# A packed attention layout without copies, moved slots, late coefficients and earlier branch hints in a fused attention and two-layer kernel

## The chip, the core and the metric

The kernel runs on one core of one Trainium2 chip. The metric is device time in microseconds (us) of one execution; lower is better. The kernel before takes 646.76 us, the median of three runs (646.42 to 647.4).

## What is computed

```python
# q, k, v: 2 x 8 heads x 768 x 64; window 128, 4 sinks
keep = (pos < n_sink) | ((rel >= 0) & (rel < window))       # rel = query - key
a = softmax(where(keep, q @ k.T / 8, -1e9)); x = a @ v       # -> 1536 x 512
g = relu(x @ w_in) ** 2;  y = g @ w_out                      # first layer, d_ff 2048
h = y @ w2_in                                                # second layer
P = a0 + a1*h + a2*h**2 + a3*h**3
Q = 1 + |b0|*|h| + |b1|*h**2
out = (P / (Q + 1e-6)) @ w2_out
```

## The kernel before

**Units and groups.** Attention is cut into 24 units: two heads (one per half of the partitions) by two query blocks of 128. `GROUPS` makes four groups of tokens, of 512, 256, 256 and 512 columns, with 8, 4, 4 and 8 units. A query block is worked on in two halves of 64 queries (j = 0, 1), and each half sees a row of 224 columns: 192 keys and 32 sink keys. `pack_attention` writes, on the host, one block of inputs for each unit, in which the keys of each half stand in the order in which the half uses them (so many keys stand twice), and V stands as pieces of 128 rows: `va` for the first 128 columns of each half and `vb` for the rest. The first unit of a sequence (`blk0 == 0`) has one plain block of 128 and one such block.

**A unit's work** (`att_unit`). Scores S are eight small matmuls (L301); VectorE adds the mask and finds the extreme of each row (L310); ScalarE exponentiates (L312); VectorE and GpSimd normalize (L320); TensorE transposes T (L333); ScalarE and VectorE copy the transposes out (L335); then O, the product with V (L348): for each job of 64 queries one matmul per head, 16 in a unit with `blk0 > 0`, 10 in the others. The trace has two records for each of these fp32 matmuls. Between these steps the generator yields.

**Order.** A planner with a timeline model orders each engine's instructions; an instruction may be drawn ahead of the program's order when it is ready and its engine has room. TensorE's order is written by hand in the start and in groups 0 to 2 (`manual_schedule`, `PINNED`); the first group's eight units run ahead of everything else, with parts of the first two gemm1 steps between them. Then `group(g)` runs 16 steps f of the first layer for one group: gemm1 (L414 to 416), `act1` (L423 to 426), and with a lag of two steps gemm2 (L437, L438, L443). The units of the next group are woven in through `slot(k)`, called three times a step: `slot` calls `tick()`, and a tick advances every open unit by one yield and on each third tick opens a new one. In group 0 the ticks begin after slot 6 (`first = 6`). In these steps the score banks are PSUM banks 6 and 7, and the third gemm1 step (f = 2) of group 0 uses bank 6 too. gemm1 otherwise alternates between banks 4 and 5, so that step f needs the `act1` of step f - 2 done.

**Weights** come as 64-bit floats into three `st` buffers (L130) and are converted on ScalarE and VectorE (L139, L140, L398, L399). All loads of weights, keys and V are issued by SyncE (SP) in its queue's order; the load of V waits in that queue for the unit before to finish with its buffer (one buffer each for `va` and `vb`).

**Setup and end.** `setup` builds three masks from `n_sink` and `window`, which a small load brings (`nsw`, L195); the coefficients a and b come by two more small loads on ScalarE's queue (L196, L197), and three VectorE instructions (L595 to L597) work them up. They are used from the second layer on (`rational`, L144). The second layer runs 3 times 16 steps with a lag of three; its `act2` is a chain over ScalarE, VectorE and GpSimd (L149 to L159, L464, L465). After the last output each engine reads a flag and branches past a slow general version (L983, L984). `hints()` (L792) marks, for each engine, a hint that this branch is likely taken, behind the last instruction of that engine in the second layer; SyncE's comes behind the stores of the second of the three token blocks.

Of the kernel before, what the change touches and what calls it, by code (L numbers as in the profile page):

```python
# [10 lines left out]
F32 = mybir.dt.float32  # L11
# [8 lines left out]
P = 128  # L20
# [6 lines left out]
KP = 2 * WK + NSK  # L27
# [61 lines left out]
def pack_attention(q, k, v):  # L89
# [3 lines left out]
    for g, c, seg, _ in units():  # L93
        b, blk0, nb = seg
        first = 0 if blk0 > 0 else 2
        kq, va, vb = [], [], []
        for half in range(2):
            h = 2 * c + half
            cols = []
            for n in range(first, 2 * nb, 2):  # L100
                s = blk0 * P - P + n * D
                cols += [kT[b, h][:, s : s + WK], kT[b, h][:, :NSK], kT[b, h][:, s + D : s + D + WK]]
            cols.append(qT[b, h][:, blk0 * P : (blk0 + nb) * P])
            kq.append(np.concatenate(cols, axis=1))
        heads = [v[b, 2 * c + half] for half in range(2)]
        pad = np.zeros((NSK, D), v.dtype)
        if blk0 == 0:
            va += [x[:P] for x in heads]
        for n in range(first, 2 * nb):
            s = blk0 * P - P + n * D  # L110
            for x in heads:
                w = x[s : s + WK]
                rows = np.concatenate([w, x[:NSK]] if n % 2 == 0 else [x[:NSK], w], axis=0)
                va.append(rows[:P])
                vb.append(np.concatenate([pad, rows[P:]], axis=0))
        parts += [np.concatenate(kq, axis=0).reshape(-1), np.concatenate(va, axis=1).reshape(-1),
                  np.concatenate(vb, axis=1).reshape(-1)]
# [44 lines left out]
class Fast:  # L162
# [17 lines left out]
    def setup(self):  # L180
# [11 lines left out]
        ab = c.tile([P, 6], F32, name="ab")  # L192
        self.ab = ab
# [31 lines left out]
        v.tensor_scalar_add(rel[hi_], rel[hi_], float(NSK - D))  # L225
# [8 lines left out]
        v.tensor_copy(m2[hi_, :NSK], out[hi_, :NSK])  # L234
        v.tensor_copy(m1, m2)
        v.tensor_copy(m2[lo_, WK:], out[lo_, :NSK])
        v.tensor_tensor(m1[lo_, :NSK], m1[lo_, :NSK], out[lo_, :NSK], op=ALU.max)
        v.memset(m1[lo_, WK:], -BIG)
# [11 lines left out]
    def att_load(self, u, early, alt):  # L250
# [7 lines left out]
        self.nc.sync.dma_start(raw, self.io["att"][off : off + P * w].rearrange("(p w) -> p w", w=w))  # L258
        return raw

    def att_load_v(self, u, alt):
# [3 lines left out]
        out = []  # L265
        for n, name, tag in ((wa, "va", tags[3]), (wb, "vb", tags[4])):
            t = self.att_tile(name, n, alt=tag)
            self.nc.sync.dma_start(t, self.io["att"][off : off + P * n].rearrange("(p w) -> p w", w=n))
            off += P * n
            out.append(t)  # L270
        return out
# [6 lines left out]
    def att_unit(self, u, raws, alt):  # L278
# [49 lines left out]
        pieces = [os[i] for i in range(nb)] + [os[i] + P - NSK for i in heads]  # L328
# [11 lines left out]
        jobs = [(va, 0, 0, 0, P)] if ws[0] == P else []  # L340
        for x, i in enumerate(heads):
            for j in range(2):
                y, q0 = 2 * x + j, i * P + j * D
                jobs.append((va, y + nb - len(heads), q0, q0, D))
                jobs.append((vb, y, (nb + x) * P + j * D, q0, D))
# [133 lines left out]
    def run(self, ctx):  # L479
# [16 lines left out]
        self.lastO = {}  # L496
# [145 lines left out]
        def second(which, g, f, between=None):  # L642
# [23 lines left out]
            else:  # L666
                self.gemm2b(f, gg, acc)
                if f == NF - 1:
                    for t in range(TG2 // P):
# [13 lines left out]
                        else:  # L683
                            (A.copy if t % 2 == 0 else V.tensor_copy)(o, acc[t])
                            self.lastO[g == NT2 - 1] = nc.sync.dma_start(dst, o)
# [4 lines left out]
        def group(g):  # L690
# [3 lines left out]
            if last:  # L694
# [5 lines left out]
                self.flag()  # L700
                wload(1, 3)
# [6 lines left out]
            def slot(k):  # L708
                nonlocal pos
                first = 6 if g == 0 else -2  # L710
# [4 lines left out]
            for f in range(NF):  # L715
                if g == 0 and f < HEAD:
# [44 lines left out]
        nsec = 0  # L761
        for i in range(len(steps) + 1):
# [29 lines left out]
    def hints(self):  # L792
        E = mybir.EngineType
        for engine, op in ((E.Activation, self.lastG), (E.Pool, self.lastL), (E.DVE, self.lastR),
                           (E.PE, self.lastM), (E.SP, self.lastO[False])):
# [3 lines left out]
    def split_y(self, t, c, ys, ysp):  # L799
# [5 lines left out]
        for g, n in enumerate(GN):  # L805
# [7 lines left out]
            self.nc.gpsimd.tensor_tensor(ylo[:, c, dst], ys[g][:, c, src], yhi[:, c, dst].bitcast(F32), op=ALU.subtract)  # L813

# [20 lines left out]
class General:  # L835
# [4 lines left out]
    def segments(self):  # L840
        off, out = 0, {}
        for g, c, seg, _ in units():
            wk, wq, wa, wb = seg_dims(seg)
            views = []
            for w in (wk + wq, wa, wb):
                views.append(self.io["att"][off : off + P * w].rearrange("(p w) -> p w", w=w))
                off += P * w
            kq, va, vb = views
            b, blk0, nb = seg
            for i in range(nb):  # L850
                whole = blk0 == 0 and i == 0
                k0 = 0 if whole else (i if blk0 > 0 else 0) * KP + WK + NSK + D
# [167 lines left out]
```

## Time and profile before

| | us |
| --- | --- |
| median of three runs | 646.76 |
| the profiled execution | 643.87 |
| its span, first to last instruction | 642.1 |

| engine | busy us | share of the span |
| --- | --- | --- |
| TensorE matmul (PE) | 609.9 | 95% |
| VectorE (DVE) | 417.8 | 65% |
| ScalarE (ACT) | 417.6 | 65% |
| GpSimd (POOL) | 109.9 | 17% |

The profile's page gives shares over the whole span; the stages differ, so the readings below are taken by stretches of time. The mean granted TensorE clock is 0.997 of full speed. Loads move 60.14 MB in all. In the rows, "[x <-y]" is idle time of the engine just before an instruction and what ended it.

### The profile page before, as it was taken

How to read it: one execution, taken by the hardware profiler on the slowest of the kernel's cores; microseconds unless marked ns; L12 is line 12 of the kernel's file. 1: busy time of each engine (PE TensorE's matmuls, PEld its weight loads, DVE VectorE, ACT ScalarE, POOL GpSimd, SP SyncE). 2: the span in 40 equal slices, each digit the busy share in tenths (PEclk: the TensorE clock that was granted, in tenths of full speed). 3: DMA queues.
4: the chain of work that ended last, by engine and by line, in shares of the span. 5: the costliest groups of instructions: out<-in, count | busy, mean ns of one | idle time of the engine just before them, and what ended most of it. 6: DMA issues, size and time to landing. Idle time of an engine off the chain costs nothing.

```text
span 642.1 us, 10520 instructions
## 1 busy us (share of the span) xinstructions
PE 609.9 (95%) x3937; PEld 510.3 (79%) x3937; DVE 417.8 (65%) x852; ACT 417.6 (65%) x896; POOL 109.9 (17%) x123
## 2 busy tenths in 40 slices
PE   3677999999999999999999999999999999999995
PEld 2555777787999899998888888888888888888884
DVE  5876788623243354346666569998788787877772
ACT  3668888735454555456777768787676666766662
POOL 1220000000000011021000003443233332222221
PEclk9999999999999999999999999999999999999998
DMA  8945677621232243104565500000010000100002
GB/s 277 353 142 169 235 252 267 207 88 43 78 91 69 97 141 94 42 1 129 185 190 190 191 0 2 1 0 1 0 67 1 1 0 1 66 0 2 1 1 70
DMA packets 21947, 60.14 MB, mean 94 GB/s; under 512 B 2816, under 2 KB 5120, under 8 KB 21888
## 3 DMA queue, kind: packets, MB, share of 16 engines
q1 hardware_dynamic: 21312, 59.25, 27.4%
q8 instruction: 33, 0.54, 0.4%
q10 hardware_dynamic: 576, 0.14, 0.1%
q14 instruction: 26, 0.21, 0.1%
HBM read 56.24 MB, written 3.15 MB: 92 GB/s over the span
## 4 chain that ended last, share of the span: by engine, by line
PE 83%; ACT 8%; DVE 6%; issue 2%; DMA 1%; POOL 0%; POOLq 0%; DVEq 0%
PE b L414 13%; PE b L415 12%; PE b L416 12%; PE b L476 7%; PE b L475 7%; PE b L474 7%; PE b L437 6%; PE b L443 6%; PE b L438 6%; PE b L348 3%; ACT p L312 3%; PE b L301 2%; PE b L333 2%; ACT top L139 2%; DVE wt L140 1%
## 5 line engine op out<-in xcount | busy, mean ns | idle before, releaser
L414 PE MATMUL b<-xhi,whi 128*128 128x512 f32 (+1 forms) x320 | 112.8, 354 | 0.5 <-ACT xhi L353 0.5
L415 PE MATMUL b<-xlo,whi 128*128 128x512 f32 (+1 forms) x320 | 111.0, 347 | 0.0
L416 PE MATMUL b<-xhi,wlo 128*128 128x512 f32 (+1 forms) x320 | 111.0, 347 | 0.0
L426 DVE TENSOR_TENSOR glo<-b,ghi 128x512 fp32r<-128x512 f32 (+1 forms) x64 | 35.5, 555 | 80.5 <-ACT b L425 75.2
L437 PE MATMUL b<-ghi,whi 128*128 128x512 f32 (+1 forms) x256 | 83.6, 343 | 0.7 <-ACT ghi L424 0.7
L438 PE MATMUL b<-ghi,wlo 128*128 128x512 f32 (+1 forms) x256 | 81.9, 336 | 0.0
L465 POOL TENSOR_TENSOR glo<-t,ghi 128x512 fp32r<-128x512 f32 x34 | 45.0, 1324 | 212.9 <-ACT ghi L464 186.5
L475 PE MATMUL b<-wlo,ghi 128*128 128x512 f32 x192 | 74.7, 389 | 0.0
L474 PE MATMUL b<-whi,ghi 128*128 128x512 f32 x192 | 74.4, 389 | 0.0
L476 PE MATMUL b<-whi,glo 128*128 128x512 f32 x192 | 71.9, 389 | 0.0
L414 PEld LDWEIGHTS b<-xhi,whi 128*128 128x128 f32 x320 | 60.4, 189 | 10.1 <-issue 1.8
L312 ACT ACTIVATE p<-p,mn 128x224 f32<-128x224 f32 (+1 forms) x96 | 44.0, 459 | 34.6 <-DVE mn L310 34.6
L416 PEld LDWEIGHTS b<-xhi,wlo 128*128 128x128 f32 x320 | 60.5, 189 | 7.5
L415 PEld LDWEIGHTS b<-xlo,whi 128*128 128x128 f32 x320 | 60.5, 189 | 7.3
L320 POOL TENSOR_SCALAR p<-p,sums 128x224 f32<-128x224 f32 (+1 forms) x48 | 25.5, 542 | 234.5 <-DVE sums L316 148.6
L399 DVE TENSOR_TENSOR wlo<-wt,whi 128x512 fp32r<-128x512 f32 x64 | 44.8, 700 | 27.1 <-ACT whi L398 26.7
L398 ACT CAST whi<-wt 128x512 fp32r<-128x512 f32 x64 | 39.5, 617 | 32.8 <-PE b L415 21.1
L423 ACT ACTIVATE b<-b 128x512 f32<-128x512 f32 (+1 forms) x64 | 31.1, 488 | 45.2 <-PE b L416 45.2
L443 PE MATMUL b<-glo,whi 128*128 128x512 f32 (+1 forms) x256 | 56.2, 342 | 0.0
L437 PEld LDWEIGHTS b<-ghi,whi 128*128 128x128 f32 x256 | 48.4, 189 | 8.1 <-issue 1.7
L438 PEld LDWEIGHTS b<-ghi,wlo 128*128 128x128 f32 x256 | 48.5, 190 | 4.9
L139 ACT CAST top<-st 128x512 f16<-128x512 bf16 x64 | 49.7, 777 | 1.8 <-DVE wt L140 1.8
(126 smaller groups left out, 1264.0 us busy)
## 6 DMA issues: line engine op xcount, KB each, us to landing
st<-w SPq DMA_DIRECT2D x64, 512.0 KB, 3.6
raw<-att SPq DMA_DIRECT2D x12, 544.0 KB, 3.6
va<-att SPq DMA_DIRECT2D x16, 256.0 KB, 3.0
vb<-att SPq DMA_DIRECT2D x16, 256.0 KB, 3.9
raw_e<-att SPq DMA_DIRECT2D x4, 544.0 KB, 6.7
out<-o SPq DMA_DIRECT2D x8, 256.0 KB, 2.0
raw<-att SPq DMA_DIRECT2D x6, 336.0 KB, 3.7
va<-att SPq DMA_DIRECT2D x8, 192.0 KB, 3.8
```

What stands on the lines that cost most here:

```text
L139: nc.scalar.copy(top.bitcast(F16).rearrange("p (n w) -> p n w", w=2)[:, :, 1], head)
L312: self.lastA = A.activation(p, p, AF.Exp, scale=-1.0, bias=mn, accum_out=sums[:, k * nb + i : k * nb + i + 1])
L414: nc.tensor.matmul(h[:, :n], whi[:, cs], xhi[:, c, :n], start=(c == 0), stop=False)
L415: nc.tensor.matmul(h[:, :n], whi[:, cs], xlo[:, c, :n], start=False, stop=False)
L416: nc.tensor.matmul(h[:, :n], wlo[:, cs], xhi[:, c, :n], start=False, stop=(c == NC - 1))
L437: nc.tensor.matmul(acc[m], whi[:, ms], ghi, start=(f == 0 and not pk), stop=pk, **kw)
L438: nc.tensor.matmul(acc[m], wlo[:, ms], ghi, start=False, stop=pk, **kw)
L443: nc.tensor.matmul(acc[m], whi[:, ms], glo, start=False, stop=pk or f == NF - 1, **kw)
L465: self.lastL = nc.gpsimd.tensor_tensor(glo, t3, ghi.bitcast(F32), op=ALU.subtract)
L474: nc.tensor.matmul(acc[t], ghi[:, ts_], whi, start=(f == 0), stop=False)
L475: nc.tensor.matmul(acc[t], ghi[:, ts_], wlo, start=False, stop=False)
L476: self.lastM = nc.tensor.matmul(acc[t], glo[:, ts_], whi, start=False, stop=(f == NF - 1))
```

## The change

- **Keys** are stored once for a unit, with the 32 sinks between neighbouring blocks, so that a half's 224 columns are a window into the row: at `i * KB + j * D`, with KB = 160. A unit's key and query load shrinks from 544 to 352 KB (from 336 to 272 KB where `blk0 == 0`). The masks follow: three small additions to `rel` in place of one, and the sink columns move.
- **V** is stored as whole blocks (`va`) and mixed pieces (`vb`): 448 KB in place of 512 KB (256 in place of 320). A unit with `blk0 > 0` has 14 matmuls at L348 in place of 16, since one job of 128 queries takes the place of two of 64; the others 8 in place of 10. In groups 1 to 3 V comes as one load, into one of two buffers.
- **Slots**: `first` goes from 6 to 9 in group 0. The ticks then fall on slots 12, 14, 17, 19, 22, ... in place of 9, 12, 14, 17, 20, ...; the last one stays on slot 46.
- **a and b** are loaded by `coefficients()`, called at the beginning of group 3, on SyncE's queue; the three VectorE instructions move there too.
- **Hints**: SyncE's comes in step 12 of group 0, behind the key load that was traced last; ScalarE's and VectorE's in step 20 of the second layer's 48; GpSimd's and TensorE's stay at the last step.
- `General` reads the new layout; it does not run with these inputs.

```diff
-KP = 2 * WK + NSK
+KB = P + NSK
@@ seg_dims
-    return (2 * KP, nb * P, 4 * P, 4 * P) if blk0 > 0 else (KP, nb * P, 3 * P, 2 * P)
+    return (2 * KB + P, nb * P, 3 * P, 4 * P) if blk0 > 0 else (KB + P, nb * P, 2 * P, 2 * P)
@@ key_cols
-    return (i if blk0 > 0 else 0) * KP + j * WK, WQ
+    return (i if blk0 > 0 else 0) * KB + j * D, WQ
@@ setup
-        nc.scalar.dma_start(ab[:, 0:4], io["a"].partition_broadcast(P))
-        nc.scalar.dma_start(ab[:, 4:6], io["bb"].partition_broadcast(P))
...
-        v.tensor_scalar_add(rel[hi_], rel[hi_], float(NSK - D))
+        for rows, cs, x in ((lo_, slice(KB, WQ), NSK), (hi_, slice(0, D), -D), (hi_, slice(D + NSK, WQ), NSK - D)):
+            v.tensor_scalar_add(rel[rows, cs], rel[rows, cs], float(x))
@@ att_load_v
+        if alt:
+            out = [self.att_tile("va", wa, alt=tags[3]), self.att_tile("vb", wb, alt=tags[4])]
...
+        t = self.att_tile("vv", wa + wb, bufs=2)
+        self.nc.sync.dma_start(t, src)
+        return [t[:, :wa], t[:, wa:]]
@@ att_unit
-        pieces = [os[i] for i in range(nb)] + [os[i] + P - NSK for i in heads]
+        pieces = [os[i] + x for i in range(nb) for x in ((0, P - NSK) if i in heads else (0,))]
...
+        if blk0 > 0:
+            jobs = [(va, 0, 0, 0, D), (vb, 0, P, 0, D), (vb, 1, D, D, D), (va, 1, P + D, D, P)]
+        else:
+            jobs = [(va, 0, 0, 0, P + D)]
+        y, pp = 2 * len(heads) - 2, (len(pieces) - 2) * P
+        jobs += [(vb, y, pp + P, P, D), (vb, y + 1, pp + D, P + D, D), (va, len(heads), pp + P + D, P + D, D)]
@@ run
-        V.tensor_scalar(self.nabs, self.ab[:, 4:6], -1.0, None, op0=ALU.mult)
-        V.tensor_tensor(self.nabs, self.nabs, self.ab[:, 4:6], op=ALU.max)
-        V.tensor_scalar(self.ab[:, 0:4], self.ab[:, 0:4], -1.0, None, op0=ALU.mult)
...
                 self.flag()
+                self.coefficients()
                 wload(1, 3)
...
-                first = 6 if g == 0 else -2
+                first = 9 if g == 0 else -2
...
+                if (g, f) == (0, 12):
+                    self.hint((mybir.EngineType.SP, self.lastD))
...
+            if i == NF + 4:
+                self.hint((E.Activation, self.lastG), (E.DVE, self.lastR))
...
                 if nsec == len(steps) - 1:
-                    self.hints()
+                    self.hint((E.Pool, self.lastL), (E.PE, self.lastM))
@@ new
+    def coefficients(self):
+        nc, io = self.nc, self.io
+        V, ab, nabs = nc.vector, self.ab, self.nabs
+        nc.sync.dma_start(ab[:, 0:4], io["a"].partition_broadcast(P))
+        nc.sync.dma_start(ab[:, 4:6], io["bb"].partition_broadcast(P))
+        V.tensor_scalar(nabs, ab[:, 4:6], -1.0, None, op0=ALU.mult)
+        V.tensor_tensor(nabs, nabs, ab[:, 4:6], op=ALU.max)
+        V.tensor_scalar(ab[:, 0:4], ab[:, 0:4], -1.0, None, op0=ALU.mult)
```

## Rows read from the trace of the kernel before

**Rows 1.** Busy time by stretch: us, PE, PEld, DVE, ACT, POOL, PE clock, DMA share, GB/s.
```profile
0.00:14.00 14.00, 4.36 (x38) 2.67 (x38) 7.26 (x43) 3.94 (x12) 2.85 (x13) 1.00 0.77 258
...
500.00:600.00 100.00, 100.00 (x443) 82.81 (x442) 78.92 (x113) 67.81 (x117) 26.56 (x21) 1.00 0.03 11
...
630.00:642.10 12.10, 4.93 (x22) 3.75 (x20) 1.12 (x2) 2.04 (x4) 1.32 (x1) 0.84 0.27 92
```

**Rows 2.** Waits of the first 56 us: who waited for whom, us, times, longest.
```profile
DVE nswf L209 <- DMA nsw<-nsw: 2.8, 1, 2.8
...
PE b L301 <- DMA raw_e<-att: 2.3, 1, 2.3
...
DVE ab L597 <- DMA ab<-a: 1.0, 1, 1.0
```

**Rows 3.** Timeline of VectorE, 5.9 to 7.4 us: start, length, instruction, idle time before.
```profile
5.96 0.16 DVE L215 TENSOR_TENSOR neg<-neg,nswf 128x2 f32<-128x2 f32 x1
...
7.11 0.17 DVE L597 TENSOR_SCALAR ab<-ab 128x4 f32<-128x4 f32 x1 [0.98 <-DMA ab<-a]
7.18 0.15 DVE L216 SCALAR_TENSOR_TENSOR par<-nswf,neg 128x2 f32<-128x2 f32 x1
```

**Rows 4.** Waits from 58.5 to 62.7 us, around the first scores of group 1.
```profile
PE b L301 <- DVE glo L426: 1.9, 1, 1.9
```

**Rows 5.** Timeline, 71.5 to 74 us: act1 of step 3 and gemm1 of step 5.
```profile
71.92 0.69 DVE L426 TENSOR_TENSOR glo<-b,ghi 128x512 fp32r<-128x512 f32 x1 [0.91 <-ACT b L425]
...
73.68 0.39 PE L414 MATMUL b<-xhi,whi 128*128 128x512 f32 x1
```

**Rows 6.** Waits from 84 to 110 us.
```profile
PE b L348 <- ACT pT L335: 0.8, 1, 0.8
```

**Rows 7.** Timeline of TensorE, 160.9 to 161.6 us: a unit's product with V.
```profile
160.93 0.55 PE L348 MATMUL b<-pT,va 128*64 128x128 f32 x8
161.31 0.29 PE L348 MATMUL b<-pT,vb 128*64 128x64 f32 x4
161.43 0.29 PE L348 MATMUL b<-pT,va 128*64 128x64 f32 x4
```

**Rows 8.** Lines L984 and L1016, all engines: length in ns, first and last start.
```profile
L984 SPq EVENT_SEMAPHORE  x8: 17/17/17, 640.2 to 640.7; - x8
...
L984 ACTq COMPARE_BRANCH  x1: 68/68/68, 636.6 to 636.6; - x1
...
L1016 PEldq BRANCH_PREFETCH_HINT  x1: 45/45/45, 628.0 to 628.0; - x1
...
L1016 ACTq BRANCH_PREFETCH_HINT  x1: 50/50/50, 629.9 to 629.9; - x1
```

**Rows 9.** DMA: q8 from 628 to 629.6, q14 from 636.5, issue to landing from 630.
```profile
q8 instruction: 1, 0.02, 3.6%
...
q14 instruction: 6, 0.05, 2.6%
...
out<-ot ACTq DMA_DIRECT2D x1, 128.0 KB, 2.3
...
out<-ot SPq DMA_DIRECT2D x1, 128.0 KB, 3.9
```

**Rows 10.** Timeline, 618 to 628 us: first and last instruction of one act2.
```profile
618.65 0.69 ACT L149 ACTIVATE y<-b,nabs 128x512 f32<-128x512 f32 x1 [1.89 <-PE b L416]
...
626.58 1.30 POOL L465 TENSOR_TENSOR glo<-t,ghi 128x512 fp32r<-128x512 f32 x1 [4.14 <-PE b L475]
```

**Rows 11.** Line L130, first 160 us: the loads of weights (32 belong to the first layer).
```profile
L130 SPq DMA_DIRECT2D st<-w  x37: 327/328/330, 9.6 to 127.0; - x37
```

**Rows 12.** Tile ab, whole span: landing of its two loads.
```profile
DMA to landing us min/median/max: 5.9/5.9/6.0
```

**Rows 13.** Timeline of SyncE's queue, 13 to 17 us.
```profile
13.47 0.33 SPq L258 DMA_DIRECT2D raw_e<-att  x1
16.57 0.33 SPq L268 DMA_DIRECT2D va<-att  x1
```

More of the change, by code (lines that the diff above doesn't have):

```diff
@@ L94, in pack_attention @@
         b, blk0, nb = seg
-        first = 0 if blk0 > 0 else 2
-        kq, va, vb = [], [], []
+        first = max(blk0 - 1, 0)
+        blocks = [slice(j * P, (j + 1) * P) for j in range(first, blk0 + nb)]
+        kq, vv = [], []
         for half in range(2):
             h = 2 * c + half
[L99 to L102, printed above, removed]
+            cols = [kT[b, h][:, blocks[0]]]
+            for x in blocks[1:]:
+                cols += [kT[b, h][:, :NSK], kT[b, h][:, x]]
             cols.append(qT[b, h][:, blk0 * P : (blk0 + nb) * P])
@@ L105, in pack_attention @@
         heads = [v[b, 2 * c + half] for half in range(2)]
+        vv += [x[r] for r in blocks for x in heads]
         pad = np.zeros((NSK, D), v.dtype)
[L107 to L117, printed above, removed]
+        for r in blocks[1:]:
+            s = r.start
+            vv += [np.concatenate([pad, x[:NSK], x[s : s + D]], axis=0) for x in heads]
+            vv += [np.concatenate([x[s - D : s], x[:NSK], pad], axis=0) for x in heads]
+        parts += [np.concatenate(kq, axis=0).reshape(-1), np.concatenate(vv, axis=1).reshape(-1)]
     return np.ascontiguousarray(np.concatenate(parts))
@@ L233, in setup @@
         v.tensor_tensor(m2, m2, fut, op=ALU.min)
-        v.tensor_copy(m2[hi_, :NSK], out[hi_, :NSK])
+        sk = slice(P, KB)
+        v.tensor_copy(m2[hi_, D : D + NSK], out[hi_, :NSK])
         v.tensor_copy(m1, m2)
-        v.tensor_copy(m2[lo_, WK:], out[lo_, :NSK])
         v.tensor_tensor(m1[lo_, :NSK], m1[lo_, :NSK], out[lo_, :NSK], op=ALU.max)
-        v.memset(m1[lo_, WK:], -BIG)
+        v.memset(m1[lo_, sk], -BIG)
+        v.tensor_copy(m2[lo_, sk], out[lo_, :NSK])
         nu = 2 * sum(u[2][2] for u in units())
@@ L264, in att_load_v @@
         off = self.att_off[u] + P * (wk + wq)
[L265 to L271, printed above, removed]
+        src = self.io["att"][off : off + P * (wa + wb)].rearrange("(p w) -> p w", w=wa + wb)
+        if alt:
+            out = [self.att_tile("va", wa, alt=tags[3]), self.att_tile("vb", wb, alt=tags[4])]
+            self.nc.sync.dma_start(out[0], src[:, :wa])
+            self.nc.sync.dma_start(out[1], src[:, wa:])
+            return out
+        t = self.att_tile("vv", wa + wb, bufs=2)
+        self.nc.sync.dma_start(t, src)
+        return [t[:, :wa], t[:, wa:]]
     def att_tile(self, tag, n, bufs=1, alt=None):
@@ L339, in att_unit @@
         ob = self.att_bank()
[L340 to L345, printed above, removed]
+        if blk0 > 0:
[4 more added lines that the diff above has]
+        jobs += [(vb, y, pp + P, P, D), (vb, y + 1, pp + D, P + D, D), (va, len(heads), pp + P + D, P + D, D)]
         for n_, (vt, vi, pp, q0, w) in enumerate(jobs):
@@ L761, in run @@
         nsec = 0
+        E = mybir.EngineType
         for i in range(len(steps) + 1):
@@ L790, in run, with hint @@
         sp.close()
[L792 to L795, printed above, removed]
+    def hint(self, *where):
+        for engine, op in where:
             with self.tc.issue_after(op.ins):
@@ L844, in segments @@
             views = []
-            for w in (wk + wq, wa, wb):
+            for w in (wk + wq, wa + wb):
                 views.append(self.io["att"][off : off + P * w].rearrange("(p w) -> p w", w=w))
                 off += P * w
-            kq, va, vb = views
+            kq, vv = views
             b, blk0, nb = seg
             for i in range(nb):
-                whole = blk0 == 0 and i == 0
-                k0 = 0 if whole else (i if blk0 > 0 else 0) * KP + WK + NSK + D
+                j = i + (1 if blk0 > 0 else 0)
                 for half in range(2):
-                    r0 = half * D
-                    ya = half if whole else 2 * (2 * i + 1) + half
-                    yb = 2 * (2 * i + 1 if blk0 > 0 else 1) + half
-                    if blk0 == 0 and i == 1:
-                        ya = 2 * 2 + half
-                    if whole:
-                        vs = [(0, P, va[:, ya * D : ya * D + D])]
-                    else:
-                        vs = [(0, NSK, va[P - NSK :, ya * D : ya * D + D]),
-                              (NSK, P, vb[NSK:, yb * D : yb * D + D])]
-                    out[(b, 2 * c + half, blk0 + i)] = (kq[r0 : r0 + D], vs, k0, wk + i * P)
+                    r0, v0 = half * D, (2 * j + half) * D
+                    out[(b, 2 * c + half, blk0 + i)] = (kq[r0 : r0 + D], vv, j * KB, wk + i * P, v0)
         return out
```

13 lines of the change are left out of this document (5 added, 8 removed).

## The prediction

> **What bounds the kernel now.** I read the busy time by stretch first, to see where TensorE is not at work, and then the waits of just those places. In the first 14 us TensorE is busy for 4.36 us, and in the last 12.1 us for 4.93; between 500 and 600 us it is busy for all of 100.00 [rows 1]. So in the second layer only fewer or shorter matmuls would pay, and the change has none there: what can be gained lies in the start, in single stalls of the groups with attention, and behind the last matmul. Three such places carry the argument. In the start VectorE stands still for a load that nobody needs yet [rows 2, 3]. At 61.75 us TensorE waits 1.9 us with the first scores of group 1 [rows 4]. And at the end three engines are past their branch at 636.6 us but do nothing until 640.2 us [rows 8].
>
> **The change, part by part.** All terms are against the profiled execution: 643.87 us, of which 642.1 are its span. The median of the runs is 2.9 us above it, so I take the sum as a difference and subtract it from 646.76.
>
> *The loads of a and b leave the start.* VectorE works its queue in order. The instruction that prepares the mask parameters (L216) stands behind L597, which waits 0.98 us for `a`: L215 starts at 5.96, L597 at 7.11, L216 at 7.18 [rows 3]. Without L597, L216 can start when L215 ends, at 5.96 + 0.16 = 6.12; that is 1.06 us earlier. The other two instructions of the three stand in the same chain ahead of the first masked scores; at L597's own step to its successor (7.18 - 7.11 = 0.07) to its length (0.17) they are 0.14 to 0.34 us. I take 1.2 us for all. It counts in full only if nothing else is late next. What may be late next is the key load of unit 1, on which TensorE waits 2.3 us [rows 2]; that load shrinks from 544 to 352 KB and those ahead of it shrink as well, so it should come earlier by itself. The two added mask instructions cost nothing: they need no load and fall into the 2.8 us in which VectorE waits for `nsw` [rows 2]; without that cover they would cost two of about 0.17 us. The gain passes through to the end because from here on the engines hand work on without a pause for loads: the waits of the first 56 us name no other load for TensorE than those of the first two units. Bounds: 0 (another wait takes its place) to 1.7 us (the unit loads come earlier too).
>
> *Slots.* The first scores of group 1 stand in slot 9, and TensorE, whose order is fixed, waits 1.9 us there for `act1` (glo, L426) to be done with bank 6, which holds step 2 of gemm1 [rows 4]. In slot 12 the same scores stand behind a whole further step; the bank is then long free, and step 3 of gemm1 comes forward. What is late next is gemm1 of step 5: it needs the bank of step 3, whose glo ends at 71.92 + 0.69 = 72.61, and it starts at 73.68 [rows 5]. So 1.07 us of the 1.9 are free in any case. For the rest `act1` of step 3 must come earlier too; the exponentials of the unit that now comes later stood ahead of it in ScalarE's queue, so I expect part of it: 1.6 us. Later ticks move by one to three slots and meet other queues: TensorE's wait for the copied transposes, of 0.8 us [rows 6], may go or double, once for each of two units. Bounds: 1.6 us lost to 3.5 us gained.
>
> *Merged jobs in the product with V.* Two jobs of 64 queries become one of 128, and a job is a pair of heads. Pairs of 64 follow one another at 161.43 - 161.31 = 0.12 us. The eight records before hold one pair of 128 and one of 64 and take 161.31 - 160.93 = 0.38, so a pair of 128 costs at most 0.26, part of which is the start of the stream [rows 7]. The number of streamed columns stays, so the saving is 2 x 0.12 less something between 0.21 (my estimate, with 0.05 for that start) and 0.26: from +0.03 to -0.02 us for each unit. The 16 units of groups 1 to 3 lie where TensorE is the bound; 0.02 each is 0.3 us. Bounds: 0.3 lost to 0.5 gained. Smaller key loads and the second V buffer I cost at nothing: from the second unit on TensorE never waits for them [rows 2], and the V loads that hang in SyncE's queue today are there before the product is due.
>
> *Hints.* ScalarE branches at 636.6 us, and SyncE starts its eight last waits at 640.2 and is done with them at 640.7 [rows 8]. In between six instruction packets are moved on q14 [rows 9], although ScalarE was given its hint at 629.9 [rows 8]. TensorE's hint at 628.0 [rows 8] was followed by a fetch on q8 within 1.6 us [rows 9]. [...] If the branch target is then there, SyncE's last wait ends with the last store: issued at 635.90, 3.9 us to landing, so 639.8 in place of 640.7, a gain of 0.9 us. That last store may itself be late because of the fetches beside it: the 128 KB of ScalarE's queue took 2.3 us [rows 9], which would bring 1.6 us more. I take 0.9. Bounds: 0 to 2.5. [...]
>
> [...]
>
> *Sum:* 1.2 + 1.6 + 0.3 + 0.9 = 4.0 us. The profiled execution would come to 639.9, the median to 646.76 - 4.0 = **642.8 us**.
>
> **The rivals.**
> 1. *The hints bring nothing*: the target is not kept, or one of the three engines still fetches, and SyncE waits for that one. For it: the fetches after the branch in spite of a hint [rows 8, 9]. Against: the same hint works on TensorE. Then 0.9 us are missing: 643.7.
> 2. *ScalarE sets the pace in group 0*: TensorE comes forward at slot 9 only to wait for `act1` from step 5 on, or the moved ticks meet longer waits. For it: the spare time there is 1.07 us [rows 5]. Against: the moved unit's exponentials leave just that queue. Then 1.6 us are missing: 644.4.
> 3. *The loads of a and b are not late.* The planner draws instructions ahead: 37 loads of weights are issued in the first 127 us, though the first layer has 32, so five of group 3's are drawn far forward [rows 11]. Those need a free buffer; the loads of a and b need nothing. SyncE's queue has nothing to issue between 13.47 + 0.33 and 16.57 us [rows 13], and two small loads put there would land behind some megabytes, with VectorE's three instructions drawn forward to where the plan expects them. The price is VectorE's wait, from 0 up to the 5.9 us that these loads take to land today [rows 12], in a stretch in which the engines wait for each other. At 3 us the whole is 645.8 and not to be told from no change; it decides from 642.8 + 5.3 on, and at its full price gives 642.8 + 5.9 = **648.7**, slower than before. Against: the plan of today errs by only 1.0 us on the same loads [rows 2].
> 4. *Gains end in other waits*: rivals 1 and 2 together and half of the start, leaving 0.9 us: 645.9.
>
> **How the numbers follow.** A measurement of this kernel can tell some 0.2%, 1.3 us, from no change. The forecast has 0.40, rival 1 0.15, rival 2 0.14, rival 3 0.20 (of that 0.04 with a small wait that still leaves it faster, 0.06 near no change, 0.10 at the upper end), rival 4 0.11. Faster: 0.40 + 0.15 + 0.14 + 0.04 = 0.73, less 0.02 for the upper ends of rival 2: 0.71. Same: 0.06 + 0.11 + 0.02 = 0.19. Slower: 0.10. The range leaves out the slower case and the last tenth below: it goes from 640.3 (the forecast with 1.6 us more at the end and 0.9 more in the slots and the start) to 646.8.
>
> **What would show it.** In the trace after: L216 of VectorE at about 6.1 us with no wait for `ab` ahead of it, and the three coefficient instructions far from the start (rival 3: they stand before 30 us, behind a wait for a load); no wait of the first scores of group 1 for glo, and gemm1 of step 5 about 2.8 us earlier than 73.68; 14 and 8 matmuls for a unit at L348; no q14 packets between the last branch and the last store's landing, and SyncE's eight waits spread out and ending with that landing, not in one run at 640.2. Wrong would make it above all a plan that differs from today's in the start, where the order is the planner's, and a wait for a load behind coefficients that were meant to be late.

## The result: faster by 6.8 us, and where they came from

| | before | after |
| --- | --- | --- |
| median, us | 646.59 (645.54 to 647.4, 4 runs) | 639.75 (638.87 to 640.31, 4 runs) |
| profiled execution, us | 643.87 | 640.31 |
| its span, us | 642.1 | 638.5 |
| mean granted TensorE clock in it | 0.997 | 0.987 |
| busy TensorE / VectorE / ScalarE, us | 609.9 / 417.8 / 417.6 | 614.0 / 417.3 / 416.9 |
| moved, MB | 60.14 | 54.86 |

The ratio is 0.9894, with a 95% interval of 0.9875 to 0.9912. I had said faster, 642.8 us with a range from 640.3 to 646.8; the direction was right, and the median lies 0.6 us under the range. The two profiled spans differ by 3.6 us only, because the execution of before from which I worked had a high granted clock and was 2.7 us under the median of 646.59; that of after had a low one and was the slowest of its four. This difference between executions of one and the same kernel turned out to be part of the story.

Busy time by stretch, kernel after; it answers [rows 1] (span us, then PE, PEld, DVE, ACT, POOL busy, granted clock, DMA share, GB/s).
```profile
0.00:14.00 14.00, 5.68 (x44) 3.35 (x46) 7.97 (x46) 6.09 (x19) 2.80 (x13) 1.00 0.81 277
500.00:600.00 100.00, 100.00 (x443) 82.81 (x442) 78.88 (x113) 66.37 (x114) 26.77 (x21) 1.00 0.03 11
626.40:638.50 12.10, 6.69 (x30) 5.21 (x28) 2.59 (x5) 2.17 (x4) 1.31 (x1) 0.87 0.26 91
```
The second layer is as full as before, as foreseen. TensorE does more in the first 14 us (5.68 against 4.36), and in the last 12.1 us it is busy 6.69 in place of 4.93: the part behind the last matmul is 1.7 us shorter (5.4 in place of 7.1 us).

The granted clock of 1.00 in the first row is not what TensorE ran at. This is a unit's set of 16 score matmuls in the kernel before:
```profile
8.93 1.77 PE L301 MATMUL b<-raw_e 64*64 64x224 f32 x16 [2.26 <-DMA raw_e<-att]
```
The same set takes 0.99 us at 22.78 us in that trace, and 1.77 us again at 34.05 us in the kernel after, where the granted clock is 0.50 (from 32 to 37 us). So by its lengths TensorE begins at about half clock, and the column shows 1.00 there all the same. The mean clock does not count that time as slow either: the 0.003 that the mean of 0.997 lacks are 1.9 of 642.1 us, and the last stretch alone lacks as much (0.16 of 12.1 us).

The start, kernel after: VectorE's first steps and the three coefficient instructions, in the timeline (start, length, instruction, idle before); they answer [rows 3].
```profile
5.71 0.16 DVE L208 TENSOR_TENSOR neg<-neg,nswf 128x2 f32<-128x2 f32 x1
5.91 0.16 DVE L209 SCALAR_TENSOR_TENSOR par<-nswf,neg 128x2 f32<-128x2 f32 x1
...
7.94 0.29 DVE L307 CUSTOM_DVE_ANT_0 p<-b,m 128x128 f32<-128x128 f32 x1
...
19.93 0.16 DVE L819 TENSOR_SCALAR ab<-ab 128x4 f32<-128x4 f32 x1
20.01 0.16 DVE L817 TENSOR_SCALAR nabs<-ab 128x2 f32<-128x2 f32 x1
...
20.20 0.16 DVE L818 TENSOR_TENSOR nabs<-nabs,ab 128x2 f32<-128x2 f32 x1
```
And who waited in its first 56 us (who for whom: us, times, longest), against [rows 2]; first of TensorE's waits, then of all engines':
```profile
PE b L298 <- DMA raw_e<-att: 0.7, 1, 0.7
```
```profile
POOL p L317 <- DVE nabs L818: 4.8, 1, 4.8
```
The wait for `ab` is gone, L209 starts at 5.91, and TensorE's wait for the keys of unit 1 is 0.7 in place of 2.3 us. But the loads of a and b did not go far: the planner drew them and their three instructions forward to 20 us. That was the premise of rival 3. Its price did not come: VectorE has no wait ahead of the three. GpSimd's wait is put down to the last of them, but that ends only 0.1 us behind the reciprocal that GpSimd needs.

The end, kernel after, lines L979 and L1011 (length in ns; first and last start), and the DMA of 633 to 638.5 us (count or KB, us from issue to landing); they answer [rows 8, 9].
```profile
L979 SPq EVENT_SEMAPHORE  x8: 17/17/17, 634.9 to 637.1; - x8
...
L979 SPq COMPARE_BRANCH  x1: 70/70/70, 634.4 to 634.4; - x1
...
L979 ACTq COMPARE_BRANCH  x1: 68/68/68, 634.7 to 634.7; - x1
...
L979 ACTq EVENT_SEMAPHORE  x1: 17/17/17, 635.2 to 635.2; - x1
...
L1011 SPq BRANCH_PREFETCH_HINT  x1: 45/45/45, 101.2 to 101.2; - x1
...
L1011 ACTq BRANCH_PREFETCH_HINT  x1: 50/50/50, 481.6 to 481.6; - x1
```
```profile
q14 instruction: 3, 0.02, 1.4%
...
out<-ot SPq DMA_DIRECT2D x1, 128.0 KB, 3.0
```
ScalarE goes on 0.5 us behind its branch; before, SyncE's eight waits began 3.6 us behind ScalarE's branch. SyncE's waits are spread out from 634.9 to 637.1 and end with the landing of the last store. That store takes 3.0 us in place of 3.9, but this is no sign of the change: in a second trace of the kernel before (its run stands below) it takes 2.8.
```profile
out<-ot SPq DMA_DIRECT2D x1, 128.0 KB, 2.8
```

### The profile page after: what moved, and what is told of

It is laid out like the page before. It is cut to its first block, busy times and chain, and to the rows that moved or that the text cites. A ratio compares the mean times of both kernels' runs of the same rounds, so it can differ in the third digit from the quotient of the medians.

```text
span 638.5 us, 10295 instructions
## 1 busy us (share of the span) xinstructions
PE 614.0 (96%) x3841; PEld 513.2 (80%) x3841; DVE 417.3 (65%) x854; ACT 416.9 (65%) x896; POOL 109.1 (17%) x123
## 2 busy tenths in 40 slices
DMA packets 19351, 54.86 MB, mean 86 GB/s; under 512 B 2528, under 2 KB 3808, under 8 KB 19296
## 4 chain that ended last, share of the span: by engine, by line
PE 92%; ACT 3%; DVE 3%; DMA 1%; issue 0%; POOL 0%; POOLq 0%
PE b L411 14%; PE b L413 13%; PE b L412 13%; PE b L434 7%; PE b L440 7%; PE b L435 7%; PE b L473 7%; PE b L472 7%; PE b L471 7%; PE b L345 4%; PE b L298 3%; PE b L330 2%; ACT p L309 2%; DVE p L307 1%; DMA nsw<-nsw 1%
```

## The experiments

All ratios are against the kernel before on the same chip, with a 95% interval. There its median was 645.73, 646.27 and 645.62 us in the three sets of runs.

### Hints: three kernels

The changed kernel with the hints at their old places:
```diff
-                if (g, f) == (0, 12):
-                    self.hint((mybir.EngineType.SP, self.lastD))
...
-            if i == NF + 4:
-                self.hint((E.Activation, self.lastG), (E.DVE, self.lastR))
...
-                    self.hint((E.Pool, self.lastL), (E.PE, self.lastM))
+                    self.hint((E.Activation, self.lastG), (E.Pool, self.lastL), (E.DVE, self.lastR), (E.PE, self.lastM), (E.SP, self.lastO[False]))
```


> The changed kernel with the branch hints back at their old places. In the changed kernel's profile SyncE's last store is issued at 633.98 us and the span ends at 638.5, 4.5 us later; before, it was 6.2 us (635.90 to 642.1). [...] Rival (the tail is shorter because the stores are fewer or land sooner): the tail stays near 4.5 us and the median within 0.5 us of 639.75.

Measured: 641.41 us, ratio 0.9927 (0.9904 to 0.9949). Its line of last waits and branches, and its DMA of the last 12 us:
```profile
L976 SPq EVENT_SEMAPHORE  x8: 17/17/17, 638.4 to 639.0; - x8
...
L976 SPq COMPARE_BRANCH  x1: 70/70/70, 634.7 to 634.7; - x1
```
```profile
q14 instruction: 6, 0.05, 1.1%
...
out<-ot SPq DMA_DIRECT2D x1, 128.0 KB, 3.7
```
With the old places the standstill is back (634.7 to 638.4), the eight waits stand in one run, and six packets move on q14 in place of three. The last store takes 3.7 us to land, not 3.0. That this comes from the fetches beside it is not shown, and the other traces speak against it: 2.8 us beside six packets in the second trace of the kernel before, 3.7 beside three in the trace of the next kernel.

The kernel before with the new hints and nothing else (the tail, here and for the next kernel, is the time from the last matmul to the end, 7.1 us before and 5.4 after):
```diff
+                if (g, f) == (0, 12):
+                    self.hint((mybir.EngineType.SP, self.lastD))
...
+            if i == NF + 4:
+                self.hint((E.Activation, self.lastG), (E.DVE, self.lastR))
...
-                    self.hints()
+                    self.hint((E.Pool, self.lastL), (E.PE, self.lastM))
```


> The kernel before with the hints at their new places, and nothing else. [...] Rival 'the last store had to wait for something else, the changed layout thins it out': tail stays at 7 or more, 645.7.

Measured: 644.08 us, ratio 0.9965 (0.9944 to 0.9986): 2.2 us, on the old layout as well. Its last waits:
```profile
L987 SPq EVENT_SEMAPHORE  x8: 17/17/17, 641.8 to 644.5; - x8
...
L987 SPq COMPARE_BRANCH  x1: 73/73/73, 641.3 to 641.3; - x1
```
SyncE goes on 0.5 us behind its branch. The rival, that only the thinner layout lets the last store land, falls. Three packets still move on q14 in the last 12 us, as in the kernel after, and the end comes 6.2 us behind the last matmul, not 5.4 as there, with a last store of 3.7 us.

The changed kernel, with ScalarE's and VectorE's hints three steps ahead of the end in place of far ahead, behind the last packet on q14 ahead of the end (603.9 us in the kernel after); SyncE's hint stays early:
```diff
-            if i == NF + 4:
+            if i == len(steps) - 3:
                 self.hint((E.Activation, self.lastG), (E.DVE, self.lastR))
```


> [...] Rival 'only SyncE's hint counts, as SyncE holds the last waits': tail 5.4, three packets.

Measured: one execution, 638.99 us. Its line of last waits:
```profile
L979 SPq EVENT_SEMAPHORE  x8: 17/17/17, 633.1 to 635.8; - x8
...
L979 DVEq COMPARE_BRANCH  x1: 84/84/84, 632.1 to 632.1; - x1
L979 SPq COMPARE_BRANCH  x1: 70/70/70, 632.6 to 632.6; - x1
L979 ACTq COMPARE_BRANCH  x1: 68/68/68, 632.7 to 632.7; - x1
L979 DVEq EVENT_SEMAPHORE  x1: 21/21/21, 636.0 to 636.0; - x1
L979 ACTq EVENT_SEMAPHORE  x1: 17/17/17, 636.3 to 636.3; - x1
```
In this kernel the engines part. VectorE and ScalarE, with hints at 614.3 and 615.0 us, stand for 3.9 and 3.6 us behind their branches; SyncE, with the early hint, goes on after 0.5. So what a hint does here differs from engine to engine, with where it stands. SyncE, ScalarE and VectorE stand for 3.5 to 3.9 us behind the branch with the old or the late places (the kernel before, the changed kernel with old hints, this one), and for 0.5 to 0.6 with the new ones (the kernel after). Why is not shown: which engine a packet of q14 belongs to stands in no trace. A mere lead time would do for these three, if it lay between 76 us (SyncE's old hint, which left the standstill) and 153 us (ScalarE's new one). GpSimd does not fit that: its hint comes 0.7 us ahead of its branch in the kernels before and after, no packet moves on q14 between the two, and it goes on 0.7 us behind the branch. But SyncE did not wait for the other two: its eight waits end at 635.8 with the last landing, and the two engines are there shortly after. What moved the end here is SyncE's hint; for those of the other two this one execution shows no gain. The distance from the last matmul to the end is 6.1 us here, 5.4 after and 7.9 with all hints at the old places.

### Slots: undone in the one, done alone in the other

```diff
-                first = 9 if g == 0 else -2
+                first = 6 if g == 0 else -2
```


> The changed kernel with first = 6 in group 0. In the changed kernel's profile TensorE has no wait over 0.4 us between 60 and 112 us; before, such waits add up to about 4.7 us there (1.9 for glo at the first scores, 2.6 at transposes and products with V). Theory 1 (the later slots take all of them away): 4 to 5 us slower than the changed kernel, 644, and the wait of the first scores for glo is back with about 2 us. Rival (the start of group 0 comes later in that profile, so ScalarE has caught up, and the slots give only what I forecast): 1 to 2 us slower, 641 to 642.

Measured: 643.69 us, ratio 0.9964 (0.9948 to 0.998). The kernel before with 9 in place of 6, and nothing else:
```diff
-                first = 6 if g == 0 else -2
+                first = 9 if g == 0 else -2
```


> The kernel before with the slots of group 0 from 9 on instead of 6, and nothing else. Taking the slots back from the changed kernel cost about 4 us. Theory 'the slots act by themselves': about 4 us are gained here too, 641.7, and no accumulation of MoE1 comes over 8 us after the one before it. Rival 'only the stall': here the wait is 1.9 us and of it 1.6 to 1.9 come back, 643.9. Second rival 'both parts need each other' (the late ticks need the shorter product with V): no change, 645.7.

Measured: 642.11 us, ratio 0.9937 (0.9912 to 0.9963), that is 4.1 us less. In the rows, glo is the low part of a step's activations, MoE1 in my expectations is the first layer, and an accumulation of glo is the last set of matmuls of a step's gemm2. The stretch from the first of them to the last but one in the first group, as the sum of a table by stretch (PE busy comes first behind the length). The kernel before, then before with slots from 9, then after:
```profile
sum 97.60, PE 94.07 PEld 74.21 DVE 60.83 ACT 69.80 POOL 7.42; mean PE 94.07 PEld 74.21 DVE 60.83 ACT 69.80 POOL 7.42
```
```profile
sum 93.30, PE 93.28 PEld 73.91 DVE 60.45 ACT 69.25 POOL 7.41; mean PE 93.28 PEld 73.91 DVE 60.45 ACT 69.25 POOL 7.41
```
```profile
sum 93.20, PE 93.20 PEld 73.82 DVE 60.30 ACT 68.86 POOL 7.39; mean PE 93.20 PEld 73.82 DVE 60.30 ACT 68.86 POOL 7.39
```
The waits of TensorE in that stretch of the kernel before:
```profile
PE b L301 <- DVE glo L426: 1.9, 1, 1.9
PE b L348 <- ACT pT L335: 0.8, 1, 0.8
PE b L348 <- DVE pT L335: 0.5, 1, 0.5
PE b L333 <- DVE mn L310: 0.4, 1, 0.4
```
and of the changed kernel with slots from 6:
```profile
PE b L298 <- DVE glo L423: 1.9, 1, 1.9
PE b L345 <- ACT pT L332: 0.4, 1, 0.4
```
In both kernels with slots from 9 the same list is empty. TensorE stood idle for 97.60 - 94.07 = 3.5 us in that stretch; with the moved slots it is 0.0, and the busy time is 0.8 shorter as well: together 4.3 us. So not one stall was taken away but all four, and the layout has no part in it. From the first accumulation to the last matmul it is 575.8 us in both traces of the kernel before, 571.3 with slots from 9, and 571.1 to 571.2 in the kernel after and in the three others that have its slots and no fill: this part hardly depends on the execution.

### The loads of a and b back in the start

```diff
+        nc.scalar.dma_start(self.ab[:, 0:4], io["a"].partition_broadcast(P))
+        nc.scalar.dma_start(self.ab[:, 4:6], io["bb"].partition_broadcast(P))
...
+        V.tensor_scalar(self.nabs, self.ab[:, 4:6], -1.0, None, op0=ALU.mult)
+        V.tensor_tensor(self.nabs, self.nabs, self.ab[:, 4:6], op=ALU.max)
+        V.tensor_scalar(self.ab[:, 0:4], self.ab[:, 0:4], -1.0, None, op0=ALU.mult)
...
-                self.coefficients()
```


> The changed kernel with the loads of a and b and their three VectorE instructions back in the setup, on ScalarE's queue. Theory 1 (the wait of VectorE for a goes into the whole): the first masked scores are 1.0 to 1.3 us later than the changed kernel's 7.94 us, and the median 1.2 us higher, 640.9. Rival (something else in the start is late next, or the clock decides): the first masked scores are later by that, but the median stays within 0.5 us of 639.75.

Measured: 639.58 us, ratio 0.9904 (0.9882 to 0.9925), not to be told from after. VectorE's first masked score, and TensorE's first accumulation of glo in MoE1, of this kernel:
```profile
8.96 0.28 DVE L309 CUSTOM_DVE_ANT_0 p<-b,m 128x128 f32<-128x128 f32 x1
```
```profile
61.55 1.08 PE L442 MATMUL b<-glo,whi 128*128 128x512 f32 x4
```
and that accumulation in the kernel after:
```profile
61.57 1.07 PE L440 MATMUL b<-glo,whi 128*128 128x512 f32 x4
```
The first masked score is 8.96 - 7.94 = 1.0 us later, as I had reckoned; the first accumulation is at 61.6 in both. That does not show that the 1.0 us is lost on the way, as the two executions differ in TensorE's clock. At about 26 us this kernel is still 1.0 us behind (a matmul of gemm1 at 26.35 against 25.29); then after falls to half clock from 31.1 to 38.0 us and from 51.6 to 55.0, this kernel from 33.0 to 36.4 and from 43.2 to 46.6, and the distance goes to -0.8, to +1.5 and to 0.0 with these falls. The medians do not decide it either: 0.9904 and 0.9894 are 0.6 us apart, and each has an interval of more than 1 us to either side.

### The rest: the layout, and TensorE's clock in the start

The kernel before once more, for the scatter:

> The kernel before, unchanged, profiled a second time. The profile shown of it has TensorE's granted clock at 1.00 in every stretch from 14 us to 630, and took 643.87 us, 2.7 us less than the median 646.59; the changed kernel's profile has 0.88, 0.76 and 0.88 in the three stretches from 14 to 56 us. Theory 1 (the clock falls in the start of most executions of either kernel, and the profile I worked from was one without it): this profile has a granted clock below 0.95 in some of those stretches, and the execution takes 645.5 to 647.5 us. Rival (the fall belongs to the changed kernel alone, and profiled executions are simply shorter): the clock is 1.00 again and the execution takes 643.5 to 644.5 us.

Measured: 645.43 us, ratio 0.9992 (0.9977 to 1.0008), single executions from 643.95 to 647.33. The profiled one took 643.95 us, with one fall (0.77 from 34 to 41 us): the clock is as theory 1 has it, the time as the rival has it, and neither came whole.

The layout alone, that is the changed kernel with the old hints, slots from 6, and a and b in the start (the edits of the kernels above together):

> The changed kernel with old slots, old hints and the loads of a and b in the start again: what is left is the layout of keys and V, the merged products, the masks and the two V buffers. Taking the other parts back one at a time cost 1.7 (hints), about 4 (slots) and 0 (a and b), together 5.7 of the 6.8 measured; so 'parts add up' expects about 1.1 us here, 644.6. Rival 'the layout loses in the start what it gains later': 645.7, no change, with the first accumulation about 2 us later than before and the stretch from 84 to 160 us shorter by as much. My forecast on record had 0.3 us for it.

Measured: 646.33 us, ratio 0.9998 (0.998 to 1.0015). It brings nothing by itself that can be measured. Its first accumulation of glo comes 4 us later than before (62.75 against 58.78 us), but that sets the slowest of its ten executions against one of the fastest of the kernel before; the trace of the kernel before with new hints, shown below, has 63.04 with the old layout. To see what the granted clock does to the start, matmuls of zeros fill TensorE's pauses in group 0, into a bank that nobody reads:
```diff
+            def fill(m):
+                for _ in range(m):
+                    nc.tensor.matmul(fb[:, :P], self.zero, self.zero, start=True, stop=True, skip_group_check=True)
...
+                fill({1: 20, 8: 12}.get(k, 0))
                 if k:
                     with tc.high_priority(offset=HP0):
                         next(g0[k - 1])
...
+                fill({2: 28, 4: 32, 6: 8}.get(k, 0))
```
This went into the changed kernel, the layout alone and the kernel before; a second form of it has 32 more for k = 1 ahead of the product with V, and 4 in place of 8.

> The changed kernel with extra matmuls of zeros (20, 28, 32, 8 and 12 of 128 columns, into a bank that nobody reads) in the pauses of TensorE during group 0's attention. Theory 'clock': the first accumulation of MoE1 starts at 61.6 us there, against 58.8 and 59.3 before, because the granted clock falls to 0.5 three times between 20 and 56 us. If the fill keeps it at 1.0, the last product with V ends near 54 in place of 56.1, that accumulation starts near 59 and the whole is near 637.5. Rival 'hand-over': the start is paced by VectorE and ScalarE, TensorE only waits; then the clock may rise, but 61.6 and 639.7 stay. If the fill itself is in the way, both get later by up to its 3 us.

Measured: 637.28 us, ratio 0.9849 (0.9817 to 0.988), with the first accumulation at 58.29 us, as theory 'clock' had it. The clock was at half from 14.9 to 21.7 us and full from there to the last matmul.

> Old slots, old hints, a and b in the start, the changed layout, and the fill. Without the fill the layout alone made no difference (ratio 0.9998), with four falls of the granted clock in its profile against one or none of the kernel before. Theory 'the layout's gain is eaten by the falls': with the fill it is 0.5 to 1.5 us under the kernel before with the fill, near 643.0. Rival 'the layout gains nothing by itself': the same time as the kernel before with the fill, 643.9.

Measured: 640.93 us, ratio 0.9923 (0.9896 to 0.9951): 5.1 us under the kernel before with the fill, where the theory had 0.5 to 1.5.

> The kernel before with the same fill of zeros in group 0's pauses as in a_fill. There the fill took 2.5 us off, with no fall of the granted clock after 20 us. Theory 'the falls are a matter of the pauses, whatever the layout': the median comes down to that of the execution without a fall, 643.9, or a little below, and the first accumulation of MoE1 is at 58.5 to 59. Rival 'only the changed layout has them': 646, no change.

Measured: 646.03 us, ratio 1.0002 (0.9984 to 1.0019): no change, though the first accumulation is at 59.17 us. The theory missed the time; what stood in the way is said below.

> a_fill with 32 more matmuls of zeros between the first unit's transposes and its product with V (12.3 to 14.4 us, where the granted clock still falls at 14.9), and 4 in place of 8 for the unit at 40 us. If the fall at 14.9 costs the start anything, the first accumulation comes at 57 to 58 us in place of 58.3 and the whole at about 636.5. Rival 'up to 24 us the pace is VectorE's and ScalarE's' (the transposes of the third unit begin at 23.5 us in either trace): the fall goes, the time stays at 637.3.

Measured: 635.29 us, ratio 0.9843 (0.9801 to 0.9886): with a_fill the fastest kernels here, and the two are not to be told apart. In its profile the fall at 14.9 us is gone, and another stands at 39.3.

The stretch from 20 to 56 us, columns as above with the granted clock third from last, and the first accumulation of glo, one fence of each for a kernel. Before:
```profile
20.00:56.00 36.00, 27.06 (x347) 19.92 (x346) 27.76 (x95) 24.70 (x76) 7.26 (x12) 1.00 0.63 216
```
```profile
58.78 1.07 PE L443 MATMUL b<-glo,whi 128*128 128x512 f32 x4
```
After (its first accumulation, 61.57, is shown above):
```profile
20.00:56.00 36.00, 29.90 (x309) 21.92 (x309) 23.88 (x88) 20.10 (x62) 6.70 (x12) 0.81 0.48 158
```
The kernel before with new hints, which has the same order of instructions as before up to there on all engines:
```profile
20.00:56.00 36.00, 28.43 (x307) 21.30 (x307) 24.80 (x90) 20.98 (x70) 7.23 (x12) 0.91 0.55 189
```
```profile
63.04 1.07 PE L443 MATMUL b<-glo,whi 128*128 128x512 f32 x4
```
After with late hints for ScalarE and VectorE, which has the same order of instructions as after up to the second layer:
```profile
20.00:56.00 36.00, 29.03 (x316) 21.39 (x317) 25.21 (x90) 21.68 (x66) 6.71 (x12) 0.91 0.49 161
```
```profile
59.49 1.07 PE L440 MATMUL b<-glo,whi 128*128 128x512 f32 x4
```
The layout alone:
```profile
20.00:56.00 36.00, 28.72 (x283) 20.98 (x283) 24.60 (x87) 21.13 (x66) 6.71 (x12) 0.81 0.47 155
```
```profile
62.75 1.07 PE L442 MATMUL b<-glo,whi 128*128 128x512 f32 x4
```
The layout alone with fill:
```profile
20.00:56.00 36.00, 32.08 (x400) 24.64 (x399) 26.92 (x91) 24.82 (x76) 6.70 (x12) 1.00 0.57 182
```
```profile
57.33 1.07 PE L442 MATMUL b<-glo,whi 128*128 128x512 f32 x4
```
After and the kernel with late hints run the same instructions in the same order up to there: at 0.81 the first accumulation comes at 61.57, at 0.91 at 59.49. The distance between the same matmuls of the two grows to 1.4 us by 37.5 us, shrinks to 0.8 by 41 and grows to 2.0 by 54.9; it grows within after's falls, and I put the 2.1 us down to the clock. The kernel before and the one with new hints are a second pair of equal orders, on the old layout: 58.78 and 63.04. The second has two falls (0.76 from 34 to 41 us and from 41 to 48), and its scores at 23.59 us still take 1.77 us, in a stretch (20 to 27 us) that reads 1.00. So these 4.3 us come without any change of the layout. The fall is to be seen in single stages too. The 16 score matmuls of one unit, after and before:
```profile
34.05 1.77 PE L298 MATMUL b<-raw_e 64*64 64x224 f32 x16
```
```profile
33.54 0.99 PE L301 MATMUL b<-raw_e 64*64 64x224 f32 x16
```
With fill the layout alone starts the first accumulation at 57.33, 5.4 us earlier than without, and the kernel before with the same fill at 59.17. Both have one fall between 16 and 21 us and none from there to that accumulation, so the 1.8 us between them may be the layout's; it is one execution of each. Why the layout without fill is no faster is not shown: falls of the clock come with the old layout too, as the second pair shows. What the traces have is the clock beside the fill: for the layout alone 0.81 from 20 to 56 us without it and 1.00 with it.

The fill in the kernel before is not a clean counterpart. In the traces of the kernel before and of that with new hints the clock from 20 to 56 us is 0.91 to 1.00, so there was something to gain in some executions. But the fill also moved the planner's order (ScalarE's differs from 15 us on), and a copy of the transposes came late for a product with V, by my reading for that reason:
```profile
PE b L348 <- ACT pT L335: 3.2, 1, 3.2
```
That wait, from 108 to 111.3 us, is in no trace of the kernel before; from the first accumulation to the last matmul this kernel takes 579.4 us in place of 575.8. For the same reason what the fill brings is not all to be put down to the clock: it changes the order in the other kernels as well. The two pairs of equal orders above are free of that.

## Why the forecast was off, by its own steps

**The loads of a and b leave the start (1.2 us): right on VectorE, open on the way to the end.** L209 starts at 5.91 (I had said 6.12), and of the 1.4 us by which the first masked score comes earlier (9.36 to 7.94), 1.0 is this edit's, by the kernel with the early loads. At the end it is worth nothing that can be measured, and the runs do not decide between 0 and 1.2 us. What the sum left out is TensorE's clock: I had the gain pass through because the waits of the first 56 us name no other load for TensorE, but granted clock is not a wait and stands in no list of waits, and between equal orders the first accumulation differs by 2.1 and 4.3 us with it. The kernel with early loads had a somewhat higher mean clock in its executions (0.994 against 0.990), which may hide a gain.

**Slots (1.6 us, bounds -1.6 to 3.5): the step that put the time under the range.** The mechanism was right, the size was not: 4.1 us (2.4 to 5.7) by the kernel with this edit alone, and 4.3 in its trace, over my own upper bound. I followed one stall and asked what would be late next behind it (gemm1 of step 5), and took only a part of 1.9. TensorE's idle time of the whole stretch, 3.5 us, was there to be read in the table by stretch, and all of it went, and 0.8 us of busy time with it. The waits of 0.5 and 0.4 us were not in my sum at all, and the one of 0.8 stood as "may go or double". None doubled. For the one stall that I did follow, the size was near: counted from the first accumulation, gemm1 of step 5 comes 2.0 us earlier (12.9 in place of 14.9 us); the rest came later, from the waits that I had left open or out. The sign that I had named for it, gemm1 of step 5 2.8 us ahead of 73.68, did not come: it is at 74.50 in the trace after, as the start of that execution is 2.8 us later. Rival 2 falls with it: no wait for `act1` came in place of the old one.

**Merged jobs (0.3 us): about right.** The 0.05 us for the start of a stream is in the trace of the kernel before: the first pair of 64 of a unit takes 32.62 - 32.45 = 0.17 us, those behind it 0.11 to 0.12. The number of records for a unit falls from 32 and 20 to 28 and 16, as said, and from the end of the stretch above to the last matmul it is 478.3 us in place of 478.5. What the smaller loads do to the start, which I had costed at nothing, is not settled: no gain shows without the fill.

**Hints (0.9 us, bounds 0 to 2.5): right that early places take the standstill away, perhaps too small.** That the branch target is there from the new places I had assumed; no run shows how a hint acts, only how long an engine stands behind its branch. The new places are worth 2.2 us (0.9 to 3.6) on the kernel before, and ratio 0.9894 against 0.9927 on the changed one, 2.1 us. The traces show about half of that directly: from the landing of the last store to the end of the span it is 2.3 to 3.1 us in the seven traces with SyncE's old hint and 1.4 to 2.0 in the seven with the new one, in the mean 2.7 and 1.6. What I had kept out, a delay of the last store by the fetches beside it, is not borne out: it lands after 2.8 to 3.9 us with SyncE's old hint, after 2.8 to 3.7 with the new one. Rival 1 falls: it is 0.5 to 0.6 us from branch to the next instruction with an early hint, 3.5 to 3.9 with a late one. What I had held against it, that the hint works on TensorE, is not shown: in the kernel before a second packet moves on q8 behind TensorE's branch, between 632.6 and 635.0 us, and TensorE goes on at 635.0, when its last matmul is done (634.55 + 0.39). I had also read the six packets of before as moved during the standstill; three of them were, at 638.2 us, and three moved behind 640.7, when it was over. Of the signs that I had named, one was wrong: three q14 packets do move behind the last branch, but nobody waits for them.

**The sum.** By the medians the parts are 4.1 (slots alone), 2.2 (hints alone), 0 (layout alone) and 0 (a and b, undone in the changed kernel): 6.3 of the 6.8 us, each with 1 to 2 us to either side. The two terms that I under-sized make up 3.8; the one that I may have over-sized is 1.2. The two profiled executions, 3.6 us apart, differ by 4.6 us less from the first accumulation to the last matmul, 1.7 less behind it and 2.8 more ahead of it. **The range** failed for a reason of its own: I had bounds of 2.5 and 3.5 us for two terms, yet let the low end take only 1.6 + 0.9 of what lay between them and my values. Both at their bounds give 642.8 - 1.6 - 1.9 = 639.3, which would have held the time, although the slots went past theirs. Rival 3 was half true, its loads were drawn forward, and cost nothing that shows. Rival 4 did not come: slots and hints both kept their gains.

## What to carry to other kernels

Before costing one stall, read the bottleneck engine's whole idle time in that stretch: a shift in the order may free all of it, and the bound of the term is that sum. In a part with pauses compare only executions with a like granted clock, or equal orders; a difference of a few us there can come without any change of the order (2.1 and 4.3 us here). Matmuls of zeros in the pauses are a cheap test, and here a gain (635.3 and 637.3 us against 639.75), though they change the order too. An early place for a branch hint is worth a try, and first on the engine that holds the last waits: here ScalarE and VectorE stood for 3.6 and 3.9 us with a hint 18 us ahead and for 0.5 and 0.6 with one 153 us ahead, SyncE for 3.8 with one 76 us ahead and for 0.5 with one 533 us ahead.

## What the runs showed of the hardware

The granted clock differs between executions of the same kernel, and its time goes with it. Of 59 further executions of the kernel before, the five with a mean granted clock of 0.997 took 643.55 to 643.84 us, the five with 0.985 or 0.986 took 647.09 to 648.27: 3.2 us or more without any change of the code. TensorE's first set of 16 scores takes 1.77 us in the traces before and after (at 8.93 and 7.26 us), the length that such a set has at a granted clock of 0.50, while the clock column reads 1.00 there. In the profiles all falls lie in the first 70 us, where TensorE has pauses, and behind the last matmul, but for one at 112.9 us, behind the wait of 3.2 us; from 117 to 630 us none was seen. What decides whether a given pause leads to a fall stays open.

SyncE, ScalarE and VectorE stood for 3.5 to 3.9 us behind a branch with a late hint (before, old hints, late hints), at a time when output stores were under way, and for 0.5 to 0.6 behind one with an early hint (after). What a hint sets going in between is not shown.
